# One weight row block moved to a casting load, with copies swapped and zero matmuls widened, in an attention and MoE kernel

## The chip, the core and the metric

The kernel runs on one core of one Trainium2 chip. Such a core has a matrix engine (PE), a vector engine (DVE), a scalar engine (ACT), GpSimd (POOL), and SyncE (SP), which here only issues transfers. Sixteen DMA engines move data between HBM and the on-chip memory SBUF; matmul results go to eight PSUM banks. The metric is the device time of one execution in microseconds (us), given as the median of several runs.

## What is computed

The inputs are `x` (8 batches, 8 heads, 512 rows, 64 columns), a `state` (8 batches, 8 heads, 32 rows, 64 columns) and two weight matrices `w_in` (512 x 2048) and `w_out` (2048 x 512), all float32.

```python
scores = 0.125 * x @ state^T;   a  = softmax(scores);   xread = a @ state
scores2 = 0.125 * state @ x^T;  a2 = softmax(scores2);  sread = a2 @ x
y = concat([xread, sread], axis=rows)        # 544 rows a batch, 4352 in all
h = y @ w_in                                 # heads side by side: 512 columns
out = (h * sigmoid(h)) @ w_out
```

## The kernel before, in words

The kernel never forms `xread`. Because `xread @ w_in` equals `a @ (state @ w_in)`, it computes for each batch a small product W1 of the state and `w_in` (`w1_m` fills PSUM, `w1_e` copies it out), multiplies it with the transposed normalized scores `aT` (`g1`, lines 322 to 349, with SiLU on ACT into `g`), and multiplies that with `w_out` (`g2`, line 354). `G2(b, ft)` is four such matmuls, one for each 128 rows of output, into four banks; it reads row block `ft` of `w_out`, 128 rows of it, held as `w_out_sb[:, ft, :]`. Sixteen row blocks make up `w_out`; four of them are a chunk. `w_in` is taken in four chunks of 512 columns. The `sread` rows of all batches are gathered and run last as a ninth batch.

The order of all instructions is written out by hand; each engine runs its own list in that order and waits where data are missing. Batch 0 is a start phase (lines 386 to 500) in which loading, transposing, scores, softmax and the first products follow each other closely. Lines 502 to 595 finish batch 0 and prepare batch 1. From line 598 on a plan gives, for each batch, the step at which each piece of the next batch is slipped between the `g2` matmuls (`phase`).

What loads the weights is this. The first chunk of `w_in` comes in float32 on SP's queue into `w_f` (line 391) and is used in float32 (`w1f_m`), then cast. The first chunk of `w_out` comes as four loads on SP's queue, one for each row block, into the float32 tile `wo_f` (line 456); POOL casts each to bfloat16 (lines 480 to 484). The other chunks come through POOL's own queue by casting loads, which read float32 and write bfloat16: `load_wi(1)` (line 457), `load_wo(1)`, `load_wi(2)`, `load_wo(2)`, `load_wi(3)`, `load_wo(3)`, with the loads of `x` for batches 1 and 2 between them (lines 479 to 499). POOL issues these itself, in its list, between its casts and its normalizations; issuing takes it 0.57 to 0.96 us each.

`warm` (lines 377 to 382) runs matmuls on a tile of zeros, whose results nobody reads: 30 before the first real work, a few more between the pieces of the start phase. `a_T` (lines 224 to 233) transposes the normalized scores `an` on PE into PSUM and copies them to `aT`; for batch 0 in two halves, one into bank `a0` and one into `a1`, each copied by the engine named beside it. `norm_m` and `norm_g` multiply the exponentials by the reciprocals of their sums, on DVE or POOL. For batch 1 this happens at lines 549 to 554, near 30 us, next to the last chunk of W1 for batch 0 (lines 557 and 558).

Of the kernel before, what the change touches and what calls it, by code (L numbers as in the profile page):

```python
# [19 lines left out]
def kernel(  # L20
# [8 lines left out]
    nc = tc.nc  # L29
# [15 lines left out]
    wo_f = pers.tile([128, 4, DM], FP32, name="wo_f")  # L45
# [19 lines left out]
    w_out_sb = pers.tile([128, 16, DM], BF16, name="w_out_sb")  # L65
# [10 lines left out]
    wout_re = moe_w_out.rearrange("(ft p) m -> p ft m", p=128)  # L76
    wout_q = moe_w_out.rearrange("(j p c) m -> p j c m", p=128, c=4)

    def bf(name):
        return bank[name][:].bitcast(BF16)  # L80

    def cp(eng, dst, src):
        if eng == "dve":
            nc.vector.tensor_copy(dst, src)  # L84
        elif eng == "pool":
            nc.gpsimd.tensor_copy(dst, src)  # L86
        else:
            nc.scalar.activation(dst, src, func=COPY, bias=0.0)  # L88
# [5 lines left out]
    def load_x(b, eng, kt=0, n=4):  # L94
        dst = x_f[b % 2][:, ds(kt, n)].rearrange("p k h e -> p (k h) e")
        eng.dma_start(dst, x_src(b, kt, n))  # L96
# [4 lines left out]
    def load_wi(j):  # L101
        nc.gpsimd.dma_start(
            w_in_sb[:, :, ds(512 * j, 512)], win_re[:, :, ds(512 * j, 512)]
        )
# [27 lines left out]
    def st_f32(bk, e0, e1):  # L132
        v = bf(bk)[:, 0:128]
        for half, e in ((0, e0), (1, e1)):
            cp(
                e,
                sbd_f[ds(64 * half, 64)],
                v[ds(64 * half, 64)].rearrange("p (ns kt) -> p kt ns", kt=KT),
            )

    def x_T(b, kt, bk):
        v = bf(bk).rearrange("p (k c t) -> p k c t", k=2, c=4)
        for c in range(4):
            nc.tensor.transpose(
                v[:, kt % 2, c, :], x_n[b % 2][:, kt, c, ds(2, 128)], ident[:]
            )
# [26 lines left out]
    def sc(b, kt, bk):  # L173
        v = bank[bk][:].rearrange("p (k h c s) -> p k h c s", k=2, h=2, c=4)
        for c in range(4):
            nc.tensor.matmul(  # L176
                v[:, kt % 2, :, c, :],
                xT[b % 2][:, kt, c, :],
                sbd[:, b, kt, :, :],
                start=True,  # L180
                stop=True,
                skip_group_check=True,
            )

    def ex(b, kt, n, bk):
        v = bank[bk][:].rearrange("p (k q s) -> p k q s", k=2, q=8)
        nc.scalar.activation(  # L187
            en[b % 2][:, :, :, ds(kt, n), :].rearrange("p h c k s -> p k (h c) s"),
            v[:, ds(kt % 2, n)],
            func=EXP,  # L190
            bias=0.0,
            scale=SCALE,
        )
# [6 lines left out]
    def norm_m(b, eng, kt=0, n=4, h0=0, hn=2):  # L200
        e = nc.vector if eng == "dve" else nc.gpsimd
        e.tensor_tensor(  # L202
            an[b % 2][:, ds(h0, hn), :, ds(kt, n), :].rearrange("p h c k s -> p (h c) k s"),
            en[b % 2][:, ds(h0, hn), :, ds(kt, n), :].rearrange("p h c k s -> p (h c) k s"),
            rs[b % 2][:, ds(h0, hn), :, ds(kt, n)]
            .rearrange("p h c k -> p (h c) k")
            .unsqueeze(3)
            .to_broadcast([128, 4 * hn, n, NS]),
            op=MULT,
        )  # L210
# [13 lines left out]
    def a_T(b, bks):  # L224
        n = 2 // len(bks)
        for i, (bk, e) in enumerate(bks):
            v = bf(bk).rearrange("p (h c t) -> p h c t", h=2, c=4)
            for half in range(n):
                for c in range(4):
                    nc.tensor.transpose(  # L230
                        v[:, half, c, :], an[b % 2][:, i * n + half, c, :, :], ident[:]
                    )
            cp(e, aT[b % 2][:, ds(i * n, n)], v[:, ds(0, n)])
# [22 lines left out]
    def sread_c(b, bk, o=0, eng="act"):  # L256
        cp(eng, s_f[b % 2][:], bank[bk][:, ds(o, 2 * D + 2)])
# [21 lines left out]
    def w1_m(b, j, bks, kts=range(KT)):  # L279
        for kt in kts:  # L280
            for half in range(2):
                nc.tensor.matmul(  # L282
                    bank[bks[half]][ds(32 * kt, 32), :],
                    sbd[ds(64 * half, 64), b, kt, half, :],
                    w_in_sb[ds(64 * half, 64), kt, ds(512 * j, 512)],
                    start=True,
                    stop=True,
                    skip_group_check=True,
                    tile_position=(64 * half, 32 * kt),
                )  # L290
# [14 lines left out]
    def w1_e(b, j, bks, engs, c0=0, n=512):  # L305
        for half in range(2):
            dst = W1[b % 2][:, half, ds(512 * j + c0, n)]
            src = bank[bks[half]][:, ds(c0, n)]
            if j > 0:
                dst = dst.rearrange("p (c q) -> p c q", c=4)  # L310
                src = src.rearrange("p (q c) -> p c q", c=4)
            cp(engs[half], dst, src)
# [38 lines left out]
    def g2(b, tt, ft, bk, cols=(0, 512)):  # L351
        src = g[b % 2] if b < B else g_s
        c0, c1 = cols
        nc.tensor.matmul(  # L354
            bank[bk][:, c0:c1],
            src[:, ft, ds(128 * tt, 128)],
            w_out_sb[:, ft, c0:c1],
            start=(ft == 0),
            stop=(ft == 15),
            skip_group_check=True,  # L360
        )
# [15 lines left out]
    def warm(n, bk, w=128):  # L377
        for i in range(n):
            nc.tensor.matmul(
                bank[bk][:, 0:w], zeros[:, 0:128], zeros[:, 0:w], start=True, stop=True,  # L380
                skip_group_check=True,
            )

    with tc.manual_schedule():
# [10 lines left out]
        for i in range(2):  # L395
            nc.vector.memset(x_n[i][:, :, :, 1:131:129], 1.0)
        nc.scalar.preload_act_table(EXP)
        warm(30, "o0")

        XB = ("o0", "o1", "o0", "w1")  # L400
        SB = ("h0", "h1", "a0", "a1")
# [1 line left out]
        HB = ("h0", "h1")  # L403
        OB = ("w0", "w1", "o0", "o1")
        DA = ("dve", "act")
        DD = ("dve", "dve")

        def G2(b, ft):
            for tt in range(4):
                g2(b, tt, ft, OB[tt])  # L410
# [19 lines left out]
        def cast2(b, kt):  # L430
            cast_x(b, "dve", (kt,), (0,))
            cast_x(b, "pool", (kt,), (1,))
# [15 lines left out]
        st_T(0, "w0", "dve", "dve")  # L448
        cast2(0, 2)
        st_f32("w0", "act", "dve")  # L450
        warm(3, "w1")
        x_T(0, 1, XB[1])
        x_Te(0, 1, 1, XB[1], "act")
        cast2(0, 3)
        for i in range(4):
            nc.sync.dma_start(wo_f[:, i, :], wout_re[:, i, :])
        load_wi(1)
        sc(0, 0, SB[0])
        ex(0, 0, 1, SB[0])
        warm(4, "w1")  # L460
        sc(0, 1, SB[1])
        ex(0, 1, 1, SB[1])
        x_T(0, 2, XB[2])
# [4 lines left out]
        x_Te(0, 3, 1, XB[3], "dve")  # L468
        rec(0)
        norm_m(0, "pool", 0, 2)  # L470
        warm(2, "o1")
        for kt in (2, 3):
            sc(0, kt, SB[kt])
            ex(0, kt, 1, SB[kt])
# [6 lines left out]
        cp("pool", w_out_sb[:, 1, :], wo_f[:, 1, :])  # L481
        load_wi(2)
        cp("pool", w_out_sb[:, 2, :], wo_f[:, 2, :])
        cp("pool", w_out_sb[:, 3, :], wo_f[:, 3, :])
        load_x(1, nc.gpsimd, 0, 2)
        warm(1, "o1", 512)
        sread_m(0, "o0")
# [1 line left out]
        warm(2, "o1", 512)  # L489
        nc.scalar.preload_act_table(SILU)  # L490
        w1_e(0, 0, ("w0", "w1"), ("act", "dve"), 0, 256)
        a_T(0, (("a0", "dve"), ("a1", "act")))
        sread_c(0, "o0", 0, "dve")
        cp("act", st_nat[:, 1, :], st_f[1][:])
        load_x(1, nc.gpsimd, 2, 2)
# [53 lines left out]
        norm_s(1, 0, 2)  # L549
        norm_m(1, "pool", 0, 2)  # L550
        nc.vector.tensor_reduce(rs[1][:, :, :, 2:4], en[1][:, :, :, 2:4, :], axis=AX, op=ADD)
        nc.vector.reciprocal(rs[1][:, :, :, 2:4], rs[1][:, :, :, 2:4])
        norm_g(1, "dve", 2, 2, 0, 5)
        norm_g(1, "pool", 2, 2, 5, 3)
        G2(0, 9)
        G2(0, 10)
        w1_m(0, 3, HB)
        w1_e(0, 3, HB, ("act", "act"))
        G2(0, 11)
        sread_m(1, "a0")  # L560
        g1(0, 12)
# [39 lines left out]
        def add(step, *fs):  # L601
            fill.setdefault(step if isinstance(step, tuple) else int(step), []).extend(fs)

        def L(f, *a):
            return lambda: f(*a)
# [52 lines left out]
        for b, (sx, ss, sq, se, tl, sr_, sg, dg) in plan.items():  # L658
            if sx is not None:
                add(sx, L(x_Td, b))  # L660
                add(ss, L(x_nu, b), L(st_T, b, "a0", "dve", "dve"))
            if 3 < b + 1 < B:
                add(sx or 74, *(L(load_x, b + 1, nc.sync, kt, 2) for kt in (0, 2)))
            add(sq, L(scs, b, 0))
            add(sq + 2, L(scs, b, 1))
            add(se, L(soft, b))
            add((tl,), L(tiled, b, tl))
            for i, q in enumerate(reads[b]):
                add(sr_ + 3 * i, L(sread_x, q, tl))
            for i in range(16):  # L670
                add(sg + dg * i, L(g1, b, i))
# [54 lines left out]
```

The softmax here doesn't subtract the row's maximum and nothing guards it: scores larger than these inputs give would overflow.

## Time and profile before

| | us |
|---|---|
| median of 4 runs | 215.85 |
| lowest and highest run | 215.38, 216.97 |
| the profiled execution, its own time | 215.99 |
| its span in the profile | 214.2 |
| PE busy in the span | 205.9 |
| ACT busy | 135.7 |
| DVE busy | 85.4 |
| POOL busy | 45.0 |

The profile is one execution. Its page has the busy time of each engine, a row of 40 slices for each engine and for the DMA engines (each digit a tenth of the slice), the chain of work that ended last, and groups of instructions. The timeline lists instructions in order of time: start, duration, engine, line of the kernel, operation, tile written and tile read, count, and in brackets how long the engine stood idle before and what ended that. PEld is the loading of weights into PE and overlaps PE. A line of the stretches gives the window, its length, the busy time and the count of instructions of PE, PEld, DVE, ACT and POOL, the granted clock of PE, the DMA share and the GB/s moved. Line numbers can be those of a helper: L354 is the matmul of `g2`, L329 that of `g1`, L282 that of `w1_m`, L379 that of `warm`, L84, L86 and L88 are copies on DVE, POOL and ACT.

### The profile page before, as it was taken

Reading aid. Unit: us, or ns where it says so; the run is one execution under the profiler, and the core shown is the slowest. Engines: PE = TensorE matmul, PEld = TensorE weight load, DVE = VectorE, ACT = ScalarE, POOL = GpSimd, SP = SyncE. Lnnn points to the kernel's source line nnn. Section 1 sums busy time; section 2 is a strip of 40 time slices with the busy share of each in tenths; the row PEclk is TensorE's granted clock in tenths of the full one; section 3 lists DMA queues with packets and bytes.
Section 4 is the critical chain, followed back from the end, with each engine's and each line's share of the span. In section 5 each row is a group of like instructions: output and inputs, shape, how many; then the busy total and the mean of one; then the engine's idle time right before and its main releaser. Section 6 shows DMA issues by size and latency. Waiting matters only on the chain.

```text
span 214.2 us, 4102 instructions
## 1 busy us (share of the span) xinstructions
PE 205.9 (96%) x1640; PEld 103.6 (48%) x1666; DVE 85.4 (40%) x183; ACT 135.7 (63%) x227; POOL 45.0 (21%) x86
## 2 busy tenths in 40 slices
PE   7799999999999999999999999999999999999993
PEld 6443444454444444544444544444454444566553
DVE  4883657805801664077015740382027611111110
ACT  4865595789587668883887477945885576233211
POOL 3767239002500430043004300160001000000000
PEclk9999999999999999999999999999999999999999
DMA  6999997692690188119910782155014111111112
GB/s 196 292 270 263 246 280 93 150 295 93 150 280 14 54 181 263 49 49 155 288 49 0 192 223 84 49 157 137 3 49 101 54 45 49 52 49 49 49 52 98
DMA packets 36803, 27.86 MB, mean 130 GB/s; under 512 B 22064, under 2 KB 31152, under 8 KB 36784
## 3 DMA queue, kind: packets, MB, share of 16 engines
q1 hardware_dynamic: 31872, 21.63, 36.0%
q0 software_dynamic: 4208, 5.44, 12.1%
q10 hardware_dynamic: 704, 0.52, 0.7%
q8 instruction: 13, 0.21, 0.4%
q14 instruction: 6, 0.05, 0.1%
HBM read 17.30 MB, written 8.91 MB: 122 GB/s over the span
## 4 chain that ended last, share of the span: by engine, by line
PE 84%; DMA 7%; ACT 3%; SPq 2%; issue 1%; POOL 1%; DVE 0%
PE ps_o L354 26%; PE ps_w L354 25%; PE ps_h L329 24%; DMA w_in_sb<-in_moe_w_in_dram 4%; PE ps_h L341 3%; DMA wo_f<-in_moe_w_out_dram 3%; PE ps_a L176 1%; SPq L96 1%; PE ps_o L282 1%; ACT W L88 1%; PE ps_h L282 1%; POOL w_out_sb L86 1%; PE ps_a L282 1%; ACT L548 1%; PE ps_o L246 1%
## 5 line engine op out<-in xcount | busy, mean ns | idle before, releaser
L338 ACT ACTIVATE g<-ps_h 128x512 bf16<-128x512 f32 x125 | 74.1, 597 | 32.5 <-PE ps_h L329 26.9
L354 PEld LDWEIGHTS <-g 128*128 128x128 bf16 x512 | 49.0, 98 | 55.2 <-issue 2.6
L329 PE MATMUL ps_h<-aT,W 128*128 128x512 bf16 x244 | 72.3, 379 | 0.5 <-ACT W L88 0.2
L354 PE MATMUL ps_w<-w_out_sb,g 128*128 128x512 bf16 x247 | 71.8, 379 | 0.7
L354 PE MATMUL ps_o<-w_out_sb,g 128*128 128x512 bf16 x247 | 65.5, 379 | 0.4
L329 PEld LDWEIGHTS <-W 128*128 128x128 bf16 x256 | 24.3, 98 | 27.7 <-issue 1.7
L202 POOL TENSOR_TENSOR an<-en,rs 128x512 bf16<-128x512 bf16 x8 | 8.4, 1053 | 107.4 <-ACT en L187 71.3
L84 DVE COPY o_sb<-ps_w 128x512 f32<-128x512 f32 (+1 forms) x13 | 8.5, 661 | 51.5 <-PE ps_w L354 51.5
L84 DVE COPY o_sb<-ps_o 128x512 f32<-128x512 f32 x14 | 9.5, 686 | 28.6 <-PE ps_o L354 23.6
L86 POOL CAST x_u<-x_f 128x256 bf16<-128x256 f32 x44 | 17.9, 451 | 0.0
L349 ACT ACTIVATE g_s<-ps_h 128x256 bf16<-128x256 f32 x16 | 6.1, 383 | 14.0 <-PE ps_h L341 14.0
L197 DVE TENSOR_REDUCE rs<-en 128x16 f32<-128x512 bf16 x13 | 8.6, 659 | 16.0 <-ACT en L187 15.9
L341 PE MATMUL ps_h<-xsT,w_in_sb 128*128 128x256 bf16 x64 | 9.6, 273 | 0.0
L88 ACT ACTIVATE W<-ps_h 128x512 bf16<-128x512 f32 x11 | 6.5, 597 | 4.5 <-PE ps_h L282 4.5
L88 ACT ACTIVATE o_sb<-ps_o 128x512 f32<-128x512 f32 (+1 forms) x4 | 2.2, 544 | 10.3 <-PE ps_o L354 7.9
L341 PEld LDWEIGHTS <-w_in_sb 128*128 128x128 bf16 x64 | 6.9, 110 | 3.7
L187 ACT ACTIVATE en<-ps_a 128x512 bf16<-128x512 f32 (+1 forms) x16 | 8.4, 568 | 0.5 <-PE ps_a L176 0.4
L84 DVE CAST W<-ps_h 128x512 bf16<-128x512 f32 x9 | 6.1, 682 | 4.8 <-PE ps_h L282 4.8
L176 PEld LDWEIGHTS <-xT 128*128 128x128 bf16 x128 | 5.8, 98 | 4.1 <-ACT xT L88 0.7
L187 ACT ACT_TABLE_LOAD x6 | 7.7, 1283 | 0.1
L640 ACT ACT_TABLE_LOAD x6 | 7.7, 1283 | 0.1
L88 ACT ACTIVATE o_sb<-ps_w 128x512 f32<-128x512 f32 (+1 forms) x5 | 2.7, 533 | 7.8 <-issue 6.2
(90 smaller groups left out, 171.2 us busy)
## 6 DMA issues: line engine op xcount, KB each, us to landing
out_dram<-o_sb SPq DMA_DIRECT2D x32, 256.0 KB, 2.6
x_f<-in_x_dram SPq DMA_DIRECT2D x8, 512.0 KB, 5.2
x_f<-in_x_dram SPq DMA_DIRECT2D x8, 256.0 KB, 4.6
w_in_sb<-in_moe_w_in_dram POOLq DMA_DIRECT2D x3, 512.0 KB, 9.8
w_out_sb<-in_moe_w_out_dram POOLq DMA_DIRECT2D x3, 512.0 KB, 9.3
w_f<-in_moe_w_in_dram SPq DMA_DIRECT2D x2, 512.0 KB, 6.0
wo_f<-in_moe_w_out_dram SPq DMA_DIRECT2D x4, 256.0 KB, 7.0
x_f<-in_x_dram POOLq DMA_DIRECT2D x2, 512.0 KB, 7.5
```

Source lines behind the costliest of these rows:

```text
L84: nc.vector.tensor_copy(dst, src)
L86: nc.gpsimd.tensor_copy(dst, src)
L88: nc.scalar.activation(dst, src, func=COPY, bias=0.0)
L176: nc.tensor.matmul(v[:, kt % 2, :, c, :], xT[b % 2][:, kt, c, :], sbd[:, b, kt, :, :], start=True, stop=True, skip_group_check=True,)
L187: nc.scalar.activation(en[b % 2][:, :, :, ds(kt, n), :].rearrange("p h c k s -> p k (h c) s"), v[:, ds(kt % 2, n)], func=EXP, bias=0.0, sc ...
L197: nc.vector.tensor_reduce(v, en[b % 2][:, :, :, ds(kt, n), :], axis=AX, op=ADD)
L202: e.tensor_tensor(an[b % 2][:, ds(h0, hn), :, ds(kt, n), :].rearrange("p h c k s -> p (h c) k s"), en[b % 2][:, ds(h0, hn), :, ds(kt, n), ...
L329: nc.tensor.matmul(bks[i][:], W1[b % 2][:, half, ds(128 * (f0 + i), 128)], aT[b % 2][:, half, :, :], start=(half == 0), stop=(half == 1), ...
L338: nc.scalar.activation(g[b % 2][:, f0 + i, :], bks[i][:], func=SILU, bias=0.0)
L341: nc.tensor.matmul(bk[:, 0:256], wi_cols(kt, ft), xsT[:, kt, :, :, :], start=(kt == 0), stop=(kt == KT - 1), skip_group_check=True,)
L354: nc.tensor.matmul(bank[bk][:, c0:c1], src[:, ft, ds(128 * tt, 128)], w_out_sb[:, ft, c0:c1], start=(ft == 0), stop=(ft == 15), skip_group ...
L640: nc.scalar.preload_act_table(SILU)
```

## The change

Five edits are made together.

- SP loads three row blocks of the first `w_out` chunk in float32 in place of four. The fourth comes by a casting load that POOL issues right behind `load_wi(1)`, straight into `w_out_sb[:, 3, :]`. POOL's cast of it is gone.
- The zero matmuls become fewer and wider: 30 of 128 columns become 8 of 512; 3, 4 and 2 of 128 columns become one of 256, one of 512 and one of 256.
- In `a_T(0, ...)` ACT copies the first half and DVE the second, where it was the other way round.
- For batch 1, the reciprocal and the normalization of the second half of the scores come after the last W1 chunk of batch 0 in the written order, on DVE and POOL; PE's own order stays. That chunk is copied out by DVE and ACT, one half each, where ACT copied both.
- The first of two SP loads of `x` for batch 4 is cut in two.

```diff
-        warm(30, "o0")
+        warm(8, "o0", 512)
...
-        warm(3, "w1")
+        warm(1, "w1", 256)
...
-        for i in range(4):
+        for i in range(3):
             nc.sync.dma_start(wo_f[:, i, :], wout_re[:, i, :])
         load_wi(1)
+        nc.gpsimd.dma_start(w_out_sb[:, 3, :], wout_re[:, 3, :])
         sc(0, 0, SB[0])
         ex(0, 0, 1, SB[0])
-        warm(4, "w1")
+        warm(1, "w1", 512)
...
-        warm(2, "o1")
+        warm(1, "o1", 256)
...
         cp("pool", w_out_sb[:, 2, :], wo_f[:, 2, :])
-        cp("pool", w_out_sb[:, 3, :], wo_f[:, 3, :])
         load_x(1, nc.gpsimd, 0, 2)
...
-        a_T(0, (("a0", "dve"), ("a1", "act")))
+        a_T(0, (("a0", "act"), ("a1", "dve")))
...
+        G2(0, 9)
+        G2(0, 10)
+        w1_m(0, 3, HB)
+        w1_e(0, 3, HB, DA)
         nc.vector.reciprocal(rs[1][:, :, :, 2:4], rs[1][:, :, :, 2:4])
         norm_g(1, "dve", 2, 2, 0, 5)
         norm_g(1, "pool", 2, 2, 5, 3)
-        G2(0, 9)
-        G2(0, 10)
-        w1_m(0, 3, HB)
-        w1_e(0, 3, HB, ("act", "act"))
...
-                add(sx or 74, *(L(load_x, b + 1, nc.sync, kt, 2) for kt in (0, 2)))
+                add(sx or 74, *(L(load_x, b + 1, nc.sync, kt, n) for kt, n in (((0, 1), (1, 1), (2, 2)) if b == 3 else ((0, 2), (2, 2)))))
```

## The prediction

> **What bounds the kernel now.** I read the page first: which engine is busy, and the row of slices. Then the chain of work that ended last, then the timeline of the first 35 us, then the stretches of 2 us with their DMA share.
>
> ```profile
> PE 205.9 (96%) x1640; PEld 103.6 (48%) x1666; DVE 85.4 (40%) x183; ACT 135.7 (63%) x227; POOL 45.0 (21%) x86
> DMA  6999997692690188119910782155014111111112
> ```
>
> PE is busy for 96% of the span, and its matmuls stand 0.216 us apart (128x512) nearly everywhere. So an edit can only move the end if it moves PE's work, and PE loses little. I looked at the starts of consecutive matmul records: after 11.5 us, where the real work begins without a break, only three stops are plainly more than a missing record or a fixed changeover of about 0.1 us. They are 0.59 us before 16.82, 0.35 us before 21.90 and about 0.2 us before 32.01. Together that is 1.16 us, 0.5% of the run. The chain names the cause of the second:
>
> ```profile
> 4.78 6.71 DMA wo_f<-in_moe_w_out_dram
> 11.54 0.60 POOL w_out_sb L86
> 12.17 0.70 POOL w_out_sb L86
> 12.87 8.99 DMA w_in_sb<-in_moe_w_in_dram
> 22.53 0.54 PE ps_w L354 x2
> ```
>
> From 22.5 us on the chain is PE work almost alone. Before it stands the landing of the third w_in chunk (issued 12.87, landed 21.86). The timeline shows both waits, and the POOL wait that the change removes:
>
> ```profile
> 15.35 0.75 POOL L86 CAST w_out_sb<-wo_f 128x512 bf16<-128x512 f32 x1 [1.04 <-DMA wo_f<-in_moe_w_out_dram]
> 16.05 1.50 POOL L96 DMA_DIRECT2D x_f<-in_x_dram  x2
> ...
> 16.82 0.41 PE L282 MATMUL ps_h<-w_in_sb,sbd 64*32 64x512 bf16 x8 [0.42 <-DMA w_in_sb<-in_moe_w_in_dram]
> 17.16 0.39 PE L354 MATMUL ps_w<-w_out_sb,g 128*128 128x512 bf16 x1
> ...
> 21.12 0.59 PE L354 MATMUL ps_o<-w_out_sb,g 128*128 128x512 bf16 x2
> 21.90 0.41 PE L282 MATMUL ps_h<-w_in_sb,sbd 64*32 64x512 bf16 x8 [0.18 <-DMA w_in_sb<-in_moe_w_in_dram]
> ```
>
> (The profile's 0.42 and 0.18 are smaller than 0.59 and 0.35, because it counts the modelled tail of the last matmul as busy.) Is that landing late because of its issue or because of the traffic? The DMA share (the column before GB/s) answers:
>
> ```profile
> 12.00:14.00 2.00, 2.00 (x11) 0.93 (x10) 2.00 (x5) 1.67 (x5) 1.98 (x4) 1.00 1.19 248
> 14.00:16.00 2.00, 2.00 (x17) 0.76 (x14) 1.53 (x5) 0.43 (x1) 0.96 (x2) 1.00 1.19 220
> 16.00:18.00 2.00, 1.52 (x20) 0.51 (x20) 0.71 (x2) 0.68 (x2) 2.00 (x4) 1.00 1.07 201
> 18.00:20.00 2.00, 2.00 (x11) 0.93 (x11) 1.02 (x2) 1.73 (x4) 2.00 (x4) 1.00 1.24 238
> 20.00:22.00 2.00, 1.81 (x16) 0.69 (x22) 0.00 (x0) 0.85 (x2) 0.30 (x1) 1.00 1.09 383
> ```
>
> All DMA engines are full from 12 to 22 us. The chunk lands when every byte ahead of it is through. An earlier issue buys nothing; only fewer bytes ahead of it would.
>
> **Part 1, the row block's way in.** Removed: the fourth 256 KB load on SP's queue (issued 6.70, landed 15.30), POOL's wait of 1.04 and cast of 0.75. Added: one casting DMA on POOL, behind the second w_in chunk.
> - *Bytes ahead of the third w_in chunk.* The same 256 KB are read before it, on another queue. In the trace's DMA packet records, a casting packet that reads 2 KB and writes 1 KB takes 98 ns (median), an SP packet of 2 KB takes 84 ns. The block is 128 packets, 8 for each of 16 engines: 8 x 98 = 0.78 us against 8 x 84 = 0.67 us. So the landing moves 21.86 to 21.97, **+0.11 us**. The stretches give the other end: casting traffic writes 201 to 248 GB/s, so 128 KB in about 0.58 us; plain traffic 383, so 256 KB in 0.68: -0.1 us. I take the packet rows, which are of the same kind of packet.
> - *The second w_in chunk.* It lands at 16.79 now, sharing the engines with SP's rest. With 0.67 us less of that, it lands near 16.1, and PE's first stop shrinks.
> - *The new wait.* `G2(0, 3)`, the four matmuls that read the block, starts at 17.16 and would need a block that lands 0.78 us after the chunk, near 16.9. PE could be there at 16.5 (8 matmuls and the changeover, 0.34 us, after 16.16). It waits 0.4 us and still starts 0.2 us sooner than now. Everything on PE queues behind it: `g1(0, 4)` and so on.
> - *What is late next.* From 16.82 to 21.55 PE is packed. Arriving sooner at 21.55 only lengthens the stop before the third chunk, and `G2(0, 4)` (now 19.39) needs the second w_out chunk, landed 19.26 now, 19.4 after. The gain at 16.82 is given back at 21.9.
> - *POOL.* The new issue falls at 7.92, after the w_in issue (0.94 us) and before `norm_m` (8.27, waiting for DVE). Nearest rows: the w_out issues, 0.57 to 0.60 us, and 0.75 to 0.94 for a w_in chunk. With 0.6 `norm_m` ends at 9.57 and the next normalization still starts at 9.61: nothing. With 0.94 the second half of the transposes is 0.3 us later, and the stop of 0.59 us at 16.82 covers it. The later POOL issues (x for batch 1 at 16.05, and those behind) come 1.75 us sooner, into full queues: nothing.
>
> **Part 2, the zero matmuls.** In the records the first 28 stand 107 ns apart and the last ones 56, from 4.2 us on: PE runs at half its rate until then, although the profile's granted clock says 1.00.
>
> ```profile
> 1.19 3.26 PE L379 MATMUL ps_o<-zeros 128*128 128x128 bf16 x30 [1.19 <-DVE zeros L393]
> ...
> 4.29 0.39 PE L144 MATMUL ps_o<-ident,x_n 128*128 128x128 bf16 x4
> ...
> 4.71 0.60 ACT L88 ACTIVATE xT<-ps_o 128x512 bf16<-128x512 bf16 x1 [0.51 <-PE ps_o L144]
> ```
>
> Eight of 512 columns are 4 x 107 = 427 ns each at that rate. If the rate doubles at 4.2 again, seven end at 4.18 and the eighth near 4.4; the first transposes start 0.1 us later. ACT's copy then ends at 5.42, and the scores that read it start at 5.48 anyway: nothing. If the rate doubles later, the eight end at 1.19 + 3.41 = 4.60, 0.3 us later, and that passes down ACT's chain to 11.5. The stop at 16.82 takes it. The other three edits change 384, 512 and 256 columns to 256, 512 and 256, each ahead of a stop of 0.15 to 0.5 us: nothing.
>
> The Trainium skill, TensorE: Matmul & The Clock Gate, Part 1, says that the warm-up is a budget of about 3.4 us of time and not a number of matmuls, in a window that runs freely against the kernel. Our row doubles after 3.0 us. By the rule the eight wide matmuls would mostly end at 4.60, by the row at 4.4; either way the sum stays as it is.
>
> **Part 3, swapped copies.** ACT takes the first half (0.60 us, from 10.62), DVE the second (0.42, from 10.84): done at 11.22 and 11.26, against 11.04 and 11.44. PE starts their reader at 11.51, behind `w1f_m`. Cover 0.25 us; cost nothing.
>
> **Part 4, the order around 30 us.** Now ACT copies both halves of W (30.87, 1.09 us for two), and `g1(0, 12)` waits for the second:
>
> ```profile
> 30.87 1.09 ACT L88 ACTIVATE W<-ps_h 128x512 bf16<-128x512 f32 x2
> 30.95 0.68 DVE L214 TENSOR_TENSOR an<-en,rs 128x320 bf16<-128x320 bf16 x1
> 31.25 0.75 POOL L214 TENSOR_TENSOR an<-en,rs 128x192 bf16<-128x192 bf16 x1
> ...
> 32.01 0.38 PE L329 MATMUL ps_h<-aT,W 128*128 128x512 bf16 x1 [0.22 <-ACT W L88]
> ```
>
> After: DVE copies one half when its second reduce ends (30.66 to 31.34), ACT the other (30.87 to 31.47). The wait of 0.22 goes. But DVE's reciprocal and normalization queue behind that copy: 31.37 to 31.62, then 31.66 to 32.34; POOL's share 31.70 to 32.45. The transposes of `an`, now at 32.44, could start at 32.22 and now wait to about 32.5. One wait takes the other's place: **+0.05 us**, between -0.2 (if they need not wait) and +0.3 (if POOL is slow).
>
> **Part 5, one x load cut in two.** SP's two issues at 58.56 take 1.46 us; a third adds about 0.6. The data lands near 65 and is first read at 73.76. Nothing.
>
> **Sum.** 0.11 + 0.05 = +0.16 us. The profiled execution took 215.99 us (span 214.2), 0.14 above the median 215.85 of the four runs. On the profiled run 216.15; on the median **216.0 us**.
>
> **Rivals.**
> - *The third chunk lands sooner.* In the packet records one DMA engine runs last: the second w_in chunk has its last packet at 16.49 and 15 engines are done by 15.72; one 16 KB instruction fetch stood at 12.79 for 931 ns. The change has 56 fewer PE instructions ahead of that, so the fetch moves. If the lag shrinks by 0.7, the pin is 21.2, PE is there by then, and the 0.2 us at 32 may go too: -0.7 to -0.9, **215.1 us**. Against it: the fetch moves by 1 to 1.5 us, still into full engines.
> - *All three stops go*: -1.16 us, **214.7 us**. Against it: Part 1's bytes.
> - *Slower: the new block lands late.* `G2(0, 3)` holds PE. Its slack is 0.35 us, so from a landing after 17.5 each us is one us of run time. If the engines serve it beside the second w_out chunk instead of before it, it lands near 19.3: +2.1 - 0.35, **217.6 us**. Against it: queue 0's loads land in order of issue (16.79, 19.26, 21.86, 23.27).
> - *Nothing arrives at the end* because every edit is hidden: 215.85, inside the forecast.
>
> The Trainium skill, Runtime: NRT & Kernel Launch, Instruction fetch mechanics, says that a 16 KiB refill costs one tail-bump, mostly hidden. For PE the trace agrees; for the transfer it delays, the 931 ns stand against it. By the page the first rival would have no cause.
>
> **Chances.** Forecast with the hidden case 0.60, sooner landing 0.20 (a quarter of it beyond -0.5%), all stops gone 0.08, late block 0.07, something on the clock or order not seen here 0.05 (half of it slower). Half a per cent, 1.08 us, is about what a measurement of this kernel tells from no change. Faster 0.05 + 0.08 + 0.02 = 0.15, slower 0.07 + 0.03 = 0.10, same 0.75. The range leaves out the 217.6 and part of the far ends: 214.9 to 216.8.
>
> **What would show it.** Right: PE's first DMA stop near 16.2, a new wait for w_out_sb at `G2(0, 3)`, the third chunk's landing at 21.8 to 22.1 with PE waiting there, DVE's normalization near 31.7 and transposes near 32.5. Wrong: no stop near 21.9, a stop of over 0.7 us at `G2(0, 3)`, or matmul spacings of 0.43 us after 11.5.

## The result, and the profile after

| | before | changed |
|---|---|---|
| median, us | 215.71 (79 runs) | 216.53 (51 runs) |
| lowest, highest | 215.08, 218.62 | 215.89, 217.64 |
| the profiled execution, its own time | 215.99 | 216.19 |
| its span | 214.2 | 214.4 |

The ratio is 1.003, with a 95% interval of 1.0021 to 1.0040. So the change costs 0.3%: inside the half per cent of the forecast, but with an interval that doesn't reach 1. The working had 0.16 us; the ratio makes 0.65 us, and the two medians stand 0.82 us apart.

The page shows PE as before, with fewer instructions, and thirteen transfers of instructions on a queue of their own, as before:

```profile
PE 206.6 (96%) x1613; PEld 101.5 (47%) x1638; DVE 85.5 (40%) x184; ACT 135.2 (63%) x226; POOL 44.8 (21%) x86
...
q8 instruction: 13, 0.21, 0.4%
```

In the timeline of the start, neither of the two waits for `w_in` is left. The second chunk's reader follows the matmuls before it directly, `G2(0, 3)` finds its casting load landed, and the third chunk costs PE about 0.1 us (its weight loads waited 0.44):

```profile
16.34 0.41 PE L282 MATMUL ps_a<-w_in_sb,sbd 64*32 64x512 bf16 x8
...
16.57 0.40 PE L282 MATMUL ps_h<-w_in_sb,sbd 64*32 64x512 bf16 x8
...
16.89 0.39 PE L354 MATMUL ps_w<-w_out_sb,g 128*128 128x512 bf16 x1
...
21.40 0.14 PEld L282 LDWEIGHTS <-sbd 64*32 64x32 bf16 x16 [0.44 <-DMA w_in_sb<-in_moe_w_in_dram]
21.41 0.41 PE L282 MATMUL ps_h<-w_in_sb,sbd 64*32 64x512 bf16 x8
```

PE is 0.49 us ahead of the profiled execution of before at that point (21.41 against 21.90), and 0.78 us ahead from 33.5 us on. A mark for this is the table load of ACT ahead of batch 2's exponentials: 49.11 us before, 48.34 now. Then all of the lead is lost at one place. The list of PE's waits between 11 and 60 us has a single entry:

```profile
PE ps_h L329 <- DMA aT<-an: 0.6, 1, 0.6
```

The chain names what PE waited for: the DMA transpose `a_Td(2)` (line 236) of batch 2's normalized scores.

```profile
52.41 0.74 POOL x_u L86
53.16 4.26 DMA aT<-an
57.42 0.05 issue
57.46 0.61 PE ps_h L329 x2
```

From issue to landing it takes 4.3 us here and 3.1 us in the kernel before, where PE never waits for it. By the starts of the matmul records PE stops for 0.78 us. From there to the end both executions run alike, but for 0.13 us that the changed kernel loses at three starts of `g1` up to 66 us (see e4). So the question is what makes the same transpose 1.2 us longer.

The stretches of half a microsecond show it (the DMA share and the GB/s are the last two columns). Before, the transpose's traffic runs through without a break (the 33 GB/s from 53.5 to 54.0 are one packet of 16 KB, which comes ahead of it):

```profile
53.50:54.00 0.50, 0.50 (x24) 0.11 (x7) 0.50 (x2) 0.50 (x2) 0.50 (x2) 1.00 0.12 33
...
55.00:55.50 0.50, 0.50 (x4) 0.23 (x3) 0.50 (x1) 0.50 (x2) 0.50 (x3) 1.00 0.75 154
55.50:56.00 0.50, 0.50 (x4) 0.26 (x3) 0.50 (x2) 0.09 (x1) 0.50 (x2) 1.00 1.12 211
56.00:56.50 0.50, 0.50 (x4) 0.20 (x2) 0.20 (x2) 0.00 (x0) 0.45 (x2) 1.00 1.16 275
56.50:57.00 0.50, 0.50 (x4) 0.22 (x3) 0.50 (x1) 0.00 (x0) 0.00 (x0) 1.00 1.02 389
```

In the changed kernel it begins at 54.3, freezes from about 55.1 to 56.4, and ends after that:

```profile
54.00:54.50 0.50, 0.50 (x4) 0.23 (x3) 0.50 (x2) 0.50 (x2) 0.50 (x2) 1.00 0.39 82
54.50:55.00 0.50, 0.50 (x4) 0.26 (x3) 0.50 (x2) 0.31 (x1) 0.50 (x3) 1.00 3.36 196
55.00:55.50 0.50, 0.50 (x4) 0.20 (x2) 0.40 (x1) 0.00 (x0) 0.50 (x2) 1.00 1.23 13
55.50:56.00 0.50, 0.50 (x4) 0.22 (x3) 0.29 (x1) 0.00 (x0) 0.17 (x1) 1.00 0.06 6
56.00:56.50 0.50, 0.50 (x5) 0.23 (x3) 0.45 (x2) 0.00 (x0) 0.00 (x0) 1.00 0.29 54
56.50:57.00 0.50, 0.34 (x2) 0.00 (x0) 0.49 (x2) 0.00 (x0) 0.00 (x0) 1.00 1.26 333
```

A reader should stop at 13 and 6 GB/s: sixteen engines move nearly nothing while a transfer is under way. The packet records say what stands there. One 16 KB packet of the instruction queue starts at 54.36 and holds one DMA engine for 1289 ns, to 55.65. Before, the corresponding packet stood at 53.60 to 54.56, ahead of the transpose's first packet at 55.1. The transpose is issued at 53.15 in the changed kernel and at 53.93 before, and its first packet comes 1.18 us later in both.

The transpose moves in packets of 256 bytes, and their records show who waits. Their median is 0.018 us. In the changed kernel twenty of them, begun between 54.83 and 55.15, take 1.29 to 1.59 us, and all twenty end between 56.41 and 56.45. When the instruction packet is through, at 55.65, about four packets start in 0.1 us until 56.4, against 75 to 113 before and after. That is less than a sixteenth of it, so it looks as if one engine works off what it has missed, while the others wait for it. Before, no packet of this transpose takes over 0.1 us.

**The theory (fetch).** There are thirteen such packets for some 3,300 PE instructions, that is one for about 256. The wide zero matmuls take 56 instructions off PE's list ahead of everything else, so each fetch comes later in the program. The fourth now falls among the packets of the transpose, which waits for it, and PE waits for the transpose. **The rival (cover):** the transpose can't land sooner whoever waits, and a PE that is 0.8 us ahead simply waits 0.8 us longer. A second rival: one of the other edits costs the time.

The Trainium skill, Runtime: NRT & Kernel Launch, Instruction fetch mechanics, says that instructions come in 16 KiB blocks of 256 and that crossing a block is mostly hidden. The packets' size and number agree. PE itself shows no wait for its instructions in these traces; what is not hidden is the block's packet in front of other traffic.

### The profile page after: what moved, and what is told of

Read it like the earlier page. It is cut to its first block, busy times and chain, and to the rows that moved or that the text cites. A ratio compares the mean times of both kernels' runs of the same rounds, so it can differ in the third digit from the quotient of the medians.

```text
span 214.4 us, 4059 instructions
## 1 busy us (share of the span) xinstructions
PE 206.6 (96%) x1613; PEld 101.5 (47%) x1638; DVE 85.5 (40%) x184; ACT 135.2 (63%) x226; POOL 44.8 (21%) x86
## 4 chain that ended last, share of the span: by engine, by line
PE 91%; DMA 2%; DVE 2%; issue 2%; ACT 2%; POOL 0%; POOLq 0%; ACTq 0%
PE ps_o L354 26%; PE ps_h L329 25%; PE ps_w L354 25%; PE ps_h L341 3%; DMA aT<-an 2%; PE ps_o L379 2%; PE ps_a L176 2%; PE ps_h L282 1%; PE ps_o L282 1%; PE ps_o L246 1%; PE ps_a L282 1%; ACT en L187 1%; PE ps_a L329 1%; ACT L187 1%; PE ps_w L282 1%
## 5 line engine op out<-in xcount | busy, mean ns | idle before, releaser
L84 DVE CAST W<-ps_h 128x512 bf16<-128x512 f32 x10 | 6.8, 682 | 4.0 <-PE ps_h L282 4.0
L88 ACT ACTIVATE W<-ps_h 128x512 bf16<-128x512 f32 x10 | 6.0, 598 | 3.6 <-PE ps_h L282 3.6
```

## The experiments

For each run the table gives what its profile shows of this place. "PE instructions" is the number against the kernel before; a zero matmul counts as two, its weight load and itself. "Fetch" is the start of the fourth instruction packet, counted from the issue of `a_Td(2)` (the transpose's own packets start at 1.18; a negative number is ahead of the issue); "landing" is the transpose's time from issue to landing; "stop" is PE's, from the starts of its matmuls; "rest" is the execution's own time less the mark, that is everything after 48 to 49.5 us. All in us. The ratio is against runs of the kernel before made beside each run (their medians are 215.71, 215.83 for e5 to e8 and 215.90 for e9 to e12).

| kernel | PE instructions | fetch | landing | stop | rest | median | ratio, 95% interval |
|---|---|---|---|---|---|---|---|
| before | 0 | -0.33 | 3.1 | 0 | 166.9 | 215.71 | |
| changed | -56 | +1.21 | 4.3 | 0.78 | 167.9 | 216.53 | 1.0030 (1.0021, 1.0040) |
| e1 | 0 | -0.81 | 3.1 | 0 | 167.0 | 215.98 | 1.0004 (0.9980, 1.0028) |
| e2 | -56 | +1.22 | 4.1 | 0.67 | 167.6 | 216.71 | 1.0036 (1.0011, 1.0061) |
| e3 | 0 | -0.78 | 3.1 | 0 | 167.0 | 215.75 | 1.0015 (0.9993, 1.0037) |
| e4 | 0 | -0.26 | 3.0 | 0 | 167.1 | 215.50 | 0.9988 (0.9963, 1.0013) |
| e5 | -40 | +1.25 | 4.0 | 0.51 | 167.5 | 216.39 | 1.0018 (0.9995, 1.0040) |
| e6 | -44 | +1.98 | 4.4 | 0.93 | 167.9 | 216.84 | 1.0036 (1.0011, 1.0062) |
| e7 | -12 | -0.08 | 3.0 | 0 | 167.1 | 215.93 | 0.9999 (0.9972, 1.0025) |
| e8 | -28 | +0.93 | 3.9 | 0.43 | 167.6 | 215.87 | 0.9996 (0.9975, 1.0017) |

Sorted by the fetch the table falls in two: where it starts before the transpose's issue, the landing is 3.0 to 3.1, there is no stop, and the rest is 166.9 to 167.1; where it starts 0.9 us or more behind the issue, the landing is 3.9 to 4.4, the stop is 0.43 to 0.93 and the rest 167.5 to 167.9. The packet records fall in the same two: in every kernel of the second kind, e9 and e11 below included, 18 to 21 packets of the transpose take 0.9 to 1.6 us and end within 0.05 us of each other, and in the first kind none takes over 0.3.

**e1, the changed kernel with the old zero matmuls.** The four `warm` lines as before, all else as changed:

```diff
-        warm(8, "o0", 512)
+        warm(30, "o0")
...
-        warm(1, "w1", 256)
+        warm(3, "w1")
...
-        warm(1, "w1", 512)
+        warm(4, "w1")
...
-        warm(1, "o1", 256)
+        warm(2, "o1")
```

> The changed kernel with the old, narrow zero matmuls, so PE has 56 more instructions ahead of the real work, as before. Theory (fetch): a 16 KB fetch of PE instructions comes every 256 instructions; in the changed kernel the fourth one (54.36 us) falls among the packets of the batch 2 transpose of the scores, which lands late, and PE loses 0.78 us at 57. With the old count it falls ahead of them again (near 53): no stop at 57, and the 0.78 us won by 46 us stay: about 215.0 us, ratio to before 0.996 to 0.998. Rival (cover): the transpose can't land sooner whoever waits, because a fixed transfer is ahead of it, so PE that comes 0.8 us sooner waits 0.8 us longer: the stop at 57 stays, 215.7 to 216.5, ratio 1.000 to 1.003.

The stop is gone and the transpose lands after 3.1 us; `g1(2, 0)` follows without a wait:

```profile
57.89 0.59 PE L329 MATMUL ps_h<-aT,W 128*128 128x512 bf16 x2
```

The ratio, 1.0004, is not the 0.996 to 0.998 that the theory gave, and its interval holds both accounts. The mechanism is as the theory has it; the 0.78 us lead that was to be kept wasn't there: this execution passed the mark at 49.54, later than before's 49.11.

**e2, the wide zero matmuls alone.** The same four lines the other way, in the kernel before.

> The kernel before with the wide zero matmuls alone. Theory (fetch): nothing is won at the start, the fetch moves into the transpose's packets and PE stops at 58 for 0.5 to 1.2 us: 216.2 to 217.0, ratio 1.002 to 1.006. Rival (cover): no gain at the start, so no stop: 215.7, ratio 0.999 to 1.001.

The stop is there without any lead at the mark (49.42), at 0.67 us, and the run is 0.36% slower. This ends the cover rival: PE was not early, and the transpose was late.

```profile
58.44 0.60 PE L329 MATMUL ps_h<-aT,W 128*128 128x512 bf16 x2 [0.51 <-DMA aT<-an]
```

**e3, the casting load alone.**

```diff
-        for i in range(4):
+        for i in range(3):
             nc.sync.dma_start(wo_f[:, i, :], wout_re[:, i, :])
         load_wi(1)
+        nc.gpsimd.dma_start(w_out_sb[:, 3, :], wout_re[:, 3, :])
...
-        cp("pool", w_out_sb[:, 3, :], wo_f[:, 3, :])
```

> The kernel before with the casting load of the fourth row block alone (and without its cast on POOL). Theory (fetch): PE's instruction count is as before, so no stop at 57; the second w_in chunk lands near 16.1 and the third moves by no more than 0.5 us: 215.2 to 215.9, ratio 0.998 to 1.001. Rival (the casting load costs): the third chunk lands late, 216.0 to 216.5, ratio 1.001 to 1.004.

No stop at 57, no wait for `w_out_sb`, rest 167.0. This execution passed the mark at 48.38, as early as the changed kernel's 48.34, and its transpose still landed after 3.1 us: an early PE alone makes no stop, which speaks against the cover rival once more. The median is 0.04 us from before; the interval reaches from -0.07% to +0.37%, so a cost of some tenths of a microsecond in the start can't be excluded.

**e4, the order near 30 us alone.**

```diff
+        G2(0, 9)
+        G2(0, 10)
+        w1_m(0, 3, HB)
+        w1_e(0, 3, HB, DA)
         nc.vector.reciprocal(rs[1][:, :, :, 2:4], rs[1][:, :, :, 2:4])
         norm_g(1, "dve", 2, 2, 0, 5)
         norm_g(1, "pool", 2, 2, 5, 3)
-        G2(0, 9)
-        G2(0, 10)
-        w1_m(0, 3, HB)
-        w1_e(0, 3, HB, ("act", "act"))
```

> The kernel before with the new order near 30 us alone (the chunk's copies on DVE and ACT, the second normalization behind them). By the changed kernel's profile the stop of 0.2 us before g1(0, 12) goes and the transposes behind it come 0.28 us sooner: 215.4, ratio 0.998 to 0.9995. By the prediction as put on record one wait takes the other's place: 215.75, ratio 1.000 to 1.001.

The median, 215.50, lies near the forecast 215.4; the interval doesn't exclude 1. The profile is sharper. From `w1_m(0, 3)` to the transposes of `an` PE now takes 31.54 - 29.43 = 2.11 us:

```profile
29.43 0.41 PE L282 MATMUL ps_h<-w_in_sb,sbd 64*32 64x512 bf16 x8
29.93 0.68 DVE L84 CAST W<-ps_h 128x512 bf16<-128x512 f32 x1
30.26 0.60 ACT L88 ACTIVATE W<-ps_h 128x512 bf16<-128x512 f32 x1
30.52 0.24 DVE L556 RECIPROCAL rs<-rs 128x16 f32<-128x16 f32 x1
...
30.80 0.49 DVE L214 TENSOR_TENSOR an<-en,rs 128x320 bf16<-128x320 bf16 x1
30.91 0.75 POOL L214 TENSOR_TENSOR an<-en,rs 128x192 bf16<-128x192 bf16 x1 [0.23 <-ACT W L88]
...
31.54 0.61 PE L230 MATMUL ps_a<-ident,an 128*128 128x128 bf16 x8
```

It is 2.11 in the changed kernel and in e1 too (31.66 - 29.55, 32.87 - 30.76), and 2.39 in every kernel with the old order (before 32.44 - 30.05, e2 32.75 - 30.36, e3 31.71 - 29.32). The edit wins 0.28 us at this place. Not all of it is kept: from the mark to a `g2` matmul near 73 us, less the stop, PE takes 24.14 to 24.16 us in the five kernels of the table with the new order and 24.02 to 24.03 in the other five. That gives back 0.13 us, at three starts of `g1` of about 0.04 each (59.5, 62.4 and 66.3 us in the changed kernel); why stays open.

**e5 to e8, between the two counts.** If the count of instructions decides and not the width of the zeros, steps between should fall on one side or the other. The first group as 16 of 256 columns takes the same PE time as 8 of 512 at the same rate (213 ns against 426 each in the profiles). e5 is the changed kernel with this; e6 and e7 are the kernel before with only the first group, or only the three small ones, widened; e8 is e5 with the small groups as before.

```diff
-        warm(8, "o0", 512)
+        warm(16, "o0", 256)
```

> The changed kernel with its first zero matmuls cut from 8 of 512 to 16 of 256 columns: the same columns and the same time, 16 more PE instructions (40 fewer than before in place of 56). Theory (fetch): the fourth fetch moves toward its old place by a third of the way; counted from the mark of the kernel (the last matmul group of the o_sb for tile 1, 46.2 in the changed profile) it starts near 7.7 us in place of 8.1, still overlaps the transpose's packets (7.9 to 9.4), and PE stops for 0.4 to 0.8 us at 57: 216.1 to 216.5. Rival (the wide zero matmuls themselves, by their time at the start): no difference from the changed kernel at any point, stop 0.78, 216.5.

> The kernel before with only the first zero matmuls widened (8 of 512), 44 PE instructions fewer. Theory (fetch): most of the way into the transpose's packets: a stop of 0.5 to 0.8 us at 57, 216.2 to 216.5, ratio 1.002 to 1.004. Rival (each zero edit costs its own time at the start): a stop only at the start, covered by the wait for w_in, 215.7, no stop at 57.

> The kernel before with only the three small groups of zero matmuls widened, 12 PE instructions fewer. Theory (fetch): the fetch starts about 0.4 us later than before, near 6.9 on the same scale, and ends at or before 8.0, ahead of the transpose's packets: no stop at 57 or under 0.2 us, 215.7 to 215.9, ratio 0.999 to 1.001. Rival: the widening itself costs, wherever: 216.0 to 216.5.

> The changed kernel with the first zero matmuls as 16 of 256 columns and the small groups as before: 28 PE instructions fewer than before. Theory (fetch): halfway; the fetch starts near 7.3 on the same scale and ends near 8.4, so it catches the first of the transpose's packets: a stop between 0 and 0.5 us, 215.7 to 216.2. Rival (width): as the changed kernel, 216.5.

The stops fell on the sides that the theory gave: none at -12, 0.43 at -28, 0.51 at -40, 0.93 at -44, 0.67 to 0.78 at -56. Three details did not fit. The stop of e6, 0.93, and its time, 216.84, lie above the 0.5 to 0.8 us and the 216.5 expected. The fetch's start doesn't move evenly with the count: it is +0.93, +1.25, +1.98 and +1.21 at -28, -40, -44 and -56. And e8 is no slower than before although it stops for 0.43 us; its profiled execution passed the mark early, at 48.01. Whether its start is faster on the whole stays open.

**e9 to e12, the reader moved away.** If the late transpose is the price, PE should not pay it when its reader comes later. The plan's step for the first products of batch 2 was moved from 110 to 113, 0.65 us of other matmuls; in the changed kernel (e9), in the kernel before as a control (e10), in e8 (e11), and in e4 (e12).

```diff
-            2: (None, None, 70, (4,), 5, 111, 110, 1.2),
+            2: (None, None, 70, (4,), 5, 111, 113, 1.2),
```

> The changed kernel with the first products of batch 2 started three steps of the plan later (step 113 in place of 110), so that three more g2 matmuls, 0.65 us, stand between the transpose's issue and its reader on PE. Nothing else changes, the fetch still falls into the transpose's packets. Theory (fetch delays the transpose, and the reader's place sets the price): the stop of 0.78 shrinks to about 0.1 us, time left after the batch 2 exponentials' table load 167.0 to 167.3 in place of 167.9: 215.8, ratio 1.000 to 1.001. Rival (the fetch holds PE itself, or the wide zeros cost elsewhere): the stop stays at 0.6 to 0.8 us, 216.5.

> The kernel before with the same three steps: the control. Its transpose lands in time, so no stop goes and nothing should change: 215.7, ratio 0.999 to 1.001. If the shift itself costs or wins, it shows here.

> The changed kernel with the first zero matmuls as 16 of 256 columns, the small groups as before, and the first products of batch 2 three steps later: the start as the changed kernel's parts allow it, without the stop of 0.43 us. Theory: 215.3 to 215.6, ratio 0.997 to 0.999. Rival (the start's edits win nothing on average): 215.7 to 215.9, ratio 0.999 to 1.001.

> The kernel before with the new order near 30 us and the same three steps later. The order alone gave 215.5 against 215.7 (interval 0.9963 to 1.0013). Theory: a gain of 0.2 to 0.3 us stays, ratio 0.998 to 0.9995; rival: none, ratio 1.000.

| kernel | fetch | landing | stop at 57 | median | ratio, 95% interval |
|---|---|---|---|---|---|
| e9 | +1.80 | 4.4 | 0.25 | 217.48 | 1.0075 (1.0049, 1.0102) |
| e10 | -0.84 | 3.1 | 0 | 217.38 | 1.0071 (1.0046, 1.0097) |
| e11 | +1.23 | 3.9 | 0 | 217.07 | 1.0058 (1.0037, 1.0078) |
| e12 | -0.83 | 3.1 | 0 | 217.56 | 1.0086 (1.0055, 1.0116) |

The control did not stay where it was: the shift itself costs 0.7%. The last two products of batch 2 now stand behind batch 3's exponentials, whose two table loads ACT must finish first, and PE, which needs them at once, waits; in the kernel before ACT is through with them when the table load starts at 69.69. In e10:

```profile
70.49 1.28 ACT L640 ACT_TABLE_LOAD   x1
71.78 1.09 ACT L338 ACTIVATE g<-ps_h 128x512 bf16<-128x512 f32 x2
```

```profile
72.43 0.88 PE L354 MATMUL ps_w<-w_out_sb,g 128*128 128x512 bf16 x2 [1.34 <-ACT g L338]
```

So none of the times that were expected came, and none of the four beat either kernel. But e9 against e10 is still the test it was meant to be. Both pay for the shift, and with it the difference between the changed kernel and the kernel before shrinks from 0.3% to nothing that can be told (1.0075 and 1.0071; with six and seven runs the intervals are too wide to exclude 0.3%), though the transpose in e9 lands as late as ever, after 4.4 us. The profiles are sharper: the stop at 57 is 0.25 in place of 0.78, and the rest is 169.04 in e9 and 168.69 in e10, 0.35 us apart where the changed kernel and the kernel before are 1.0 apart. A fetch that held PE itself would not have cost less for a later reader.

## Why the prediction was right, and where it was not

The forecast, no change beyond half a per cent, held, with 216.0 us for a measured 216.53. The sum behind it was not what happened, so that the time stayed inside is luck in good part. Of the signs that the prediction named for being right none came: no DMA stop near 16.2, no wait at `G2(0, 3)`, the third chunk near 21.4 and not 21.8 to 22.1, DVE's normalization at 30.91 and the transposes at 31.66, not 31.7 and 32.5. Of its signs of being wrong the first nearly did: the stop near 21.9 is 0.1 us. What did happen lies in the 0.05 that it gave to something not seen.

- *What bounds the kernel.* That PE sets the end was right. The three stops of 1.16 us were a reading of one execution: of the first two, the 0.59 before the second chunk is absent in e1, e3, e4, e5, e7 and e8 and 0.3 in e2 and e6, and the 0.35 before the third is 0.1 in the changed kernel. The mark lies between 48.0 and 49.5 us in ten profiled executions, the rest is within 0.2 us where the transpose is on time. The start of this kernel varies by more than the forecast's terms. Median less rest gives an estimate of the usual mark: 215.71 - 166.9 = 48.8 before and 216.53 - 167.9 = 48.6 changed. So of the 0.78 us that the changed kernel led by in the two profiles, about 0.2 is usual.
- *Part 1, +0.11 us on the third chunk.* Not settled. It landed 8.6 us after its issue at 12.81, near 21.4, 0.5 sooner than before; but without the casting load its reader started at 21.29 (e4) and 21.36 (e7), with it alone at 21.17 (e3). The forecast wait at `G2(0, 3)` didn't show; its start, 16.89, is near the forecast (0.2 before 17.16).
- *Part 2, nothing.* This is the step that failed. The time at the start came as worked out: the transposes of `x` begin at 4.58 (forecast 4.4 to 4.6). What was costed at nothing was the count: 56 instructions fewer on PE. The first rival did see that the fetches would move, but looked only at the fetch at 12.79 and only for a gain. The fetch at 53.60, 0.33 us ahead of the issue of a transpose, was not looked at. It moved behind that issue, the transpose landed after 4.3 us in place of 3.1, and PE waited 0.78 us for it. The price shows in the rest, 0.5 to 1.0 us longer in five executions.
- *Part 3, nothing.* Right. ACT copies from 11.15 to 11.75, DVE from 11.37 to 11.80. PE starts the reader at 11.86, 0.6 us after `w1f_m` (11.27), as before (10.91 and 11.51), so it didn't wait for a copy. But the cover was 0.06 us, not 0.25.
- *Part 4, +0.05 us.* The first wait went, as forecast; the second, which was to take its place, didn't come, and the term was -0.28 in place of +0.05, outside its own bounds (-0.2 to +0.3). Two steps of DVE were shorter than in the sum: the reciprocal started 0.6 us after the start of the copy, before the copy's record ended, and the normalization took 0.49 in place of 0.68. Why it was faster stays open; POOL's share runs beside it for 0.38 us both times.
- *Part 5, nothing.* SP's issues took 2.12 in place of 1.46 us, and no wait for `x` followed.

That the instruction packet delays the transpose is shown by where it falls in fourteen profiles, by the packets of the transpose that wait it out, and by e1, which undoes the zero edit, and e2, which makes it alone. Why one engine held for 1.3 us keeps the others from moving the transpose's packets was not tried; nor was the fetch itself taken away, only moved, and each time by the zero matmuls.

## What to carry to other kernels

Instructions are data too: here, taking 28 to 56 of them off the head of PE's long list moved the later instruction fetches, and one that fell into a transfer with a tight reader cost more than the edit saved. Look at where the instruction packets stand beside the transfers that the critical engine waits for, not only in the stage that is edited. And before a stop in the start phase is given a price, see it in more than one execution.

## What the runs showed that was not expected

A 16 KB instruction packet takes 0.9 to 2.0 us in these runs, and a DMA transpose that met it landed 0.8 to 1.4 us later (3.9 to 4.4 against 3.0 to 3.1), in the changed kernel with all sixteen engines together at 6 to 13 GB/s for about a microsecond. In the kernel before, after the packet at 12.79, the second `w_in` chunk's packets come one at a time from 15.72 to 16.49, as if one engine ran some 0.8 us behind the others. PE's rate also doubles at a different time in each execution: with the narrow zeros the half-rate spacing ended at 4.2 us in one and after 5 us in others, with the granted clock shown as 1.00 in the kernel before all along.
